# Buffers at multiples of 512 bytes and a reordered lead-in, in a fused retention and feed-forward kernel

## The chip, the cores and the metric

The kernel runs on one core of one Trainium2 chip. The metric is device time in microseconds (us) of one execution. Every time below comes with its number of runs. Every ratio is of executions in the fast state alone, against the kernel before, run on the same chip in the same rounds. Stages and waits are read from one profiled execution of each kernel.

## The reference, cut to what matters

Eight batches of eight heads, 576 positions of 64 elements, are put through retention: scores are `q·k`, scaled by 1/8, multiplied by a decay gamma^(i-j) where i is at or after j, and multiplied with v. The result is laid out as 4608 rows of 512 and goes through `gelu(x @ w_in) @ w_out` with 2048 inner columns, where gelu is `h * sigmoid(1.702 h)`. Inputs and output are float32.

```python
scores = scale * np.matmul(q, k.transpose(0, 1, 3, 2))
ret = scores * Dmat[None, :, :, :]          # Dmat: gamma ** (i - j), 0 above the diagonal
x = np.matmul(ret, v)                       # ... transposed to (4608, 512)
h = x @ w_in
out = (h * (1.0 / (1.0 + np.exp(-1.702 * h)))) @ w_out
```

## The kernel before

The 4608 rows are 36 units of 128 rows, and four units are a chunk. Each unit has its k, q, v loaded (k and q cast to bf16 on the way), k and q transposed, scores, masked scores (`pm`), the retention state (`kv`), and x. Each chunk has `up` (w_in, 16 groups of four matmuls, gelu on ScalarE) and `down` (w_out, four output tiles of 16 matmuls). From chunk 1 on, the attention of the next units is threaded between the matmuls of the present chunk. The part before chunk 1 is the lead-in.

First, the buffers. They are allocated in the order of these lines, and small tables come first, so in the compiled program every large buffer starts 160 bytes past a multiple of 512.

```python
dmat = sb("dmat", [P, P], FP32)
ident = sb("ident", [P, P], BF16)
# ... 13 more small or middling tables ...
kqn = [sb(f"kqn{i}", [P, 2, H, DH], BF16) for i in range(NLD)]   # NLD = 12 slots
vn = [sb(f"vn{i}", [P, H, DH], FP32) for i in range(NLD)]
# ... vp, kqT, pm, kv, xT ...
w_in_sb = sb("w_in_sb", [P, 4, FF], BF16)
w_out_sb = sb("w_out_sb", [P, NF, DM], BF16)
```

Second, the lead-in, in program order (each engine takes its own instructions from it in this order):

```python
def lead_in():
    load_kq(0, 0); load_kq(0, 1); load_v(0, eng="sp")
    # ... iotas ...
    load(1); load_win(0); load(2); load(3)
    for i in range(1, 4): load_win(i)
    for i in range(4): load_wout(i)
    for u in range(4, NPE + 2): load(u)      # units 4 to 9
    warm(8)                                   # eight 512-column matmuls on zeros
    # ... tables ...
    transposes(0, "E", "B")                   # k into PSUM bank E, q into bank B
    # ... scores and block of units 0 and 1 ...
    up(0, 0, 0, 2)                            # first gelu: 256 columns, bank A
    transposes(2, "E", "B")
    up(0, 1, 0, 2)                            # bank B
    # ...
```

Third, units 8 and up are transposed by DMA instead of TensorE, and their loads are held back by that:

```python
for c in range(1, NCH):
    if c == 1:
        for u in range(10, 14):
            load(u, after=["T1_0"])           # until the DMA transpose of unit 9 has landed
    for u in range(4 * c + 6, min(4 * c + 10, NU)):
        dma_transpose(u)                      # SP queue
    for u in range(4 * c + 10, 4 * c + 14):
        load(u, after=[f"T{(4 * c + 9) % NQT}_0"])
```

The `work` table says after which quarter of which output tile of chunk 0 the attention of units 4 to 7 comes.

## Time and profile before

The median of three runs was 310.06 us (310.0 to 310.06).

| | before |
|---|---|
| TensorE (PE) busy | 296.5 us of 308.0, 96% |
| clock records (they begin at 5.0 us) | half speed from 8.4 to 28.9 us (20.48 us) |
| first `down` of chunk 0, first `up` of chunk 1 (start records) | 40.10 us, 61.99 us |
| last w_out landed | 39.05 us |
| DMA transpose of unit 13 landed; PE began the pair of units that reads it | 86.66 us; 86.8 us |

From the page of the kernel before, first the span and two rows of the 40 slices (busy tenths of PE, granted clock in tenths), then two rows of the DMA issues (times issued, KB each, median us from issue to landing):

```profile
span 308.0 us, 6292 instructions
...
PE   6779999899999999999999999999999999999996
...
PEclk9556999999999999999999999999999999999999
...
w_out_sb<-in_moe_w_out_dram POOLq DMA_DIRECT2D x4, 512.0 KB, 17.7
...
vn<-in_v_dram POOLq DMA_DIRECT2D x7, 256.0 KB, 21.4
```

Only the first four slices (31 us) are poor, in busy share and in clock. After that PE is full. The next view is of PE's waits in the first 66 us (who waited for whom: us in total, times, longest):

```profile
PE psB L572 <- ACT kqT L402: 2.2, 2, 1.5
PE psB L392 <- DMA kqn<-in_q_dram: 2.0, 2, 1.3
...
PE psC L484 <- ACT kqT L402: 1.0, 2, 0.7
PE psX L468 <- DVE kv L442: 0.7, 1, 0.7
```

The largest is an `up` (L572) that waits for copies of transposes. The timeline shows why (start, duration, engine, line, operation, and in brackets the idle time before it):

```profile
15.39 1.28 ACT L577 ACT_TABLE_LOAD   x1
...
16.68 0.38 ACT L577 ACTIVATE gT<-psA 128x256 bf16<-128x256 f32 x1
16.96 0.59 ACT L402 ACTIVATE kqT<-psE 128x512 bf16<-128x512 bf16 x1
17.27 0.69 DVE L384 TENSOR_TENSOR vp<-vn,vfac 128x512 bf16<-128x512 f32 x1 [2.77 <-DMA vn<-in_v_dram]
17.44 0.60 ACT L402 ACTIVATE kqT<-psB 128x512 bf16<-128x512 bf16 x1
...
18.10 1.03 PE L572 MATMUL psB<-xT,w_in_sb 128*128 128x256 bf16 x4 [1.50 <-ACT kqT L402]
```

The first gelu needs another activation table, the copies of unit 2 queue behind it, and bank B is not free for the second `up` until the second copy is done. Two other things matter in this stretch: v of unit 2 has just landed, and PE runs at half speed.

The loads of units 10 to 13 start when the transpose of unit 9 has landed (59.53 us), take GpSimd 5.4 us of issuing per unit, and end in the transpose of unit 13 at 86.66 us.

### The profile page before, as it was taken

To read this page: it belongs to the slowest core of one execution; us is meant where nothing else is said; L and a number is where in the kernel's file an instruction comes from. 1 tells how busy PE (TensorE), PEld (TensorE's weight loads), DVE (VectorE), ACT (ScalarE), POOL (GpSimd) and SP (SyncE) were. 2 spreads that over 40 slices of the span, in tenths; PEclk is the share of its full clock that TensorE was granted. 3 is DMA by queue.
4 is the path that set the end of the run, shared out by engine and by line. 5 is a ranking of instruction groups with operands and counts; after the bars stand their busy time and mean duration, and the time that the engine had idled before them with its cause. 6 is when DMAs were issued, how large, how long until landed. Compare 5 with 4: busy or idle time off the path is not lost.

```text
span 308.0 us, 6292 instructions
## 1 busy us (share of the span) xinstructions
PE 296.5 (96%) x2664; PEld 142.1 (46%) x2664; DVE 118.0 (38%) x246; ACT 126.2 (41%) x238; POOL 187.3 (61%) x276
## 2 busy tenths in 40 slices
PE   6779999899999999999999999999999999999996
PEld 2446545444544445445444444454445444443344
DVE  3738307845441444134424442344244424410000
ACT  5555734266115611561166116611661166116611
POOL 8999470299669949973994699489909600000000
PEclk9556999999999999999999999999999999999999
DMA  9999999899999969996999699979999760010022
GB/s 101 173 193 205 205 179 204 148 149 146 116 152 179 166 107 144 186 130 116 141 149 172 99 137 178 174 91 169 176 121 113 126 106 0 36 70 34 0 57 81
DMA packets 120396, 40.27 MB, mean 131 GB/s; under 512 B 109296, under 2 KB 113648, under 8 KB 120368
## 3 DMA queue, kind: packets, MB, share of 16 engines
q0 software_dynamic: 84368, 22.82, 71.6%
q1 hardware_dynamic: 36000, 17.05, 26.4%
q8 instruction: 21, 0.34, 0.5%
q14 instruction: 7, 0.06, 0.1%
HBM read 36.70 MB, written 9.44 MB: 150 GB/s over the span
## 4 chain that ended last, share of the span: by engine, by line
PE 92%; DVE 2%; ACT 2%; DMA 2%; POOL 1%; issue 0%; POOLq 0%
PE psA L583 21%; PE psB L572 20%; PE psA L572 20%; PE psB L583 19%; PE psK L430 3%; PE psX L468 2%; DMA kqn<-in_q_dram 2%; ACT kqT L402 1%; POOL kqn L241 1%; PE psY L536 1%; PE psC L484 1%; DVE pm L503 1%; PE psX L536 1%; PE psX L523 1%; PE psE L392 1%; PE psD L495 1%
## 5 line engine op out<-in xcount | busy, mean ns | idle before, releaser
L241 POOL DMA_DIRECT2D kqn<-in_k_dram x94 | 68.3, 807 | 52.5 <-DMA kqT<-kqn 49.5
L572 PE MATMUL psB<-xT,w_in_sb 128*128 128x512 bf16 (+1 forms) x296 | 74.8, 376 | 2.2 <-ACT kqT L402 2.2
L572 PE MATMUL psA<-xT,w_in_sb 128*128 128x512 bf16 (+1 forms) x296 | 74.9, 377 | 0.1
L259 POOL DMA_DIRECT2D vn<-in_v_dram x93 | 68.9, 854 | 3.2 <-issue 3.2
L583 PE MATMUL psA<-w_out_sb,gT 128*128 128x512 bf16 (+1 forms) x304 | 69.9, 374 | 0.0
L583 PE MATMUL psB<-w_out_sb,gT 128*128 128x512 bf16 (+1 forms) x288 | 64.2, 373 | 0.0
L241 POOL DMA_DIRECT2D kqn<-in_q_dram x70 | 57.0, 892 | 0.0
L577 ACT ACTIVATE gT<-psB 128x512 bf16<-128x512 f32 (+1 forms) x74 | 42.9, 580 | 26.9 <-PE psB L572 26.7
L442 DVE CAST kv<-psK 64x256 bf16<-64x256 f32 x56 | 23.6, 422 | 74.9 <-PE psK L430 74.3
L577 ACT ACTIVATE gT<-psA 128x512 bf16<-128x512 f32 (+1 forms) x74 | 42.9, 580 | 20.8 <-PE psA L572 20.6
L572 PEld LDWEIGHTS psA<-xT,w_in_sb 128*128 128x128 bf16 x296 | 26.0, 99 | 36.8 <-ACT gT L577 12.7
L583 PEld LDWEIGHTS psA<-w_out_sb,gT 128*128 128x128 bf16 x304 | 28.2, 98 | 31.1 <-ACT gT L577 1.0
L583 PEld LDWEIGHTS psB<-w_out_sb,gT 128*128 128x128 bf16 x288 | 27.9, 98 | 31.5
L572 PEld LDWEIGHTS psB<-xT,w_in_sb 128*128 128x128 bf16 x296 | 24.7, 99 | 32.7 <-ACT gT L577 10.5
L593 ACT ACTIVATE osb<-psA 128x512 f32<-128x512 f32 x18 | 10.7, 597 | 66.2 <-PE psA L583 66.2
L593 ACT ACTIVATE osb<-psB 128x512 f32<-128x512 f32 (+1 forms) x18 | 10.5, 586 | 48.7 <-PE psB L583 48.7
L511 DVE TENSOR_TENSOR pm<-psB,maskp 128x384 bf16<-128x384 f32 x12 | 6.7, 558 | 38.3 <-PE psB L495 38.3
L384 DVE TENSOR_TENSOR vp<-vn,vfac_s 128x512 bf16<-128x512 f32 x27 | 18.5, 689 | 1.1 <-DMA vn<-in_v_dram 0.6
L430 PE MATMUL psK<-vp,kqn 128*128 128x128 bf16 x128 | 13.3, 230 | 0.0
L430 PEld LDWEIGHTS psK<-vp,kqn 128*128 128x128 bf16 x128 | 9.7, 102 | 6.9 <-issue 0.7
L595 DVE COPY osb<-psA 128x256 f32<-128x256 f32 x1 | 0.4, 425 | 32.5 <-PE psA L583 32.5
L560 DVE TENSOR_TENSOR xT<-psX,gq 128x512 bf16<-128x512 f32 x13 | 8.9, 682 | 5.2 <-PE psX L536 5.2
(89 smaller groups left out, 230.6 us busy)
## 6 DMA issues: line engine op xcount, KB each, us to landing
out_dram<-osb SPq DMA_DIRECT2D x31, 256.0 KB, 2.7
vn<-in_v_dram POOLq DMA_DIRECT2D x60, 64.0 KB, 3.4
vn<-in_v_dram POOLq DMA_DIRECT2D x26, 128.0 KB, 3.9
kqn<-in_q_dram POOLq DMA_DIRECT2D x50, 64.0 KB, 4.2
w_in_sb<-in_moe_w_in_dram POOLq DMA_DIRECT2D x8, 256.0 KB, 9.4
w_out_sb<-in_moe_w_out_dram POOLq DMA_DIRECT2D x4, 512.0 KB, 17.7
kqn<-in_k_dram POOLq DMA_DIRECT2D x60, 32.0 KB, 3.0
vn<-in_v_dram POOLq DMA_DIRECT2D x7, 256.0 KB, 21.4
```

What stands on the lines that cost most here:

```text
L241: e.dma_start(kqn[sl][p0 : p0 + n, which, ds, :], src[b, ss, s0 : s0 + n, :].rearrange("h p d -> p h d"),)
L259: e.dma_start(vn[sl][p0 : p0 + n, ss, :], v[b, ss, s0 : s0 + n, :].rearrange("h p d -> p h d"),)
L384: op(eng, lambda e: e.tensor_tensor(vp[u % NVP].ap(), vn[sl].ap(), (vfac if u < NSW else vfac_s)[:, ty, :, None].to_broadcast([P, H, DH]), ...
L430: op("pe", lambda e, hp=hp: e.matmul(bank["K"][:, P * hp : P * hp + P], kq_pair(u, 0, hp), v_pair(u, hp), start=(c == 0 and hp == 0), stop ...
L442: op("dve", lambda e, dst=dst, src=src: e.tensor_copy(dst, src), reads=["K"], writes=[f"kv{u % NKV}_{hh}"])
L468: op("pe", lambda e, g=g, pb=pb, hh=hh, hp=hp, s=s, uv=uv, t0=t0, n=n: e.matmul(xbank(hh, slot)[64 * pb : 64 * pb + 64, g, t0 : t0 + n], k ...
L511: op("dve", lambda e: e.tensor_tensor(pm[u % 4][hh][:, 0:384].rearrange("p (a i) -> p a i", i=192), ps32(banks[hh])[:, 0:384].rearrange("p ...
L560: op("dve", lambda e: e.tensor_tensor(xT[ch % 2][:, x_tiles(u0, hh), P * jj : P * jj + 2 * P].rearrange("p g (u t) -> p u g t", u=2), ps32 ...
L572: op("pe", lambda e, a=a: e.matmul(bank[b][:, n0:n1], w_in_sb[:, a, P * f : P * f + P], xT[c % 2][:, a, n0:n1], start=(a == 0), stop=(a == ...
L577: op("act", lambda e: e.activation(gT[c % 2][:, f, n0:n1], bank[b][:, n0:n1], AF.Gelu_apprx_sigmoid), reads=[b], writes=[f"g{c % 2}_{f}_{j ...
L583: op("pe", lambda e, f=f: e.matmul(bank[b][:, 0 : n1 - n0], gT[c % 2][:, f, P * r : P * r + P], w_out_sb[:, f, n0:n1], start=(f == 0), sto ...
L593: op("act", lambda e: e.activation(dst, src, AF.Copy), reads=[b], writes=[f"osb{i}_{n0}"])
```

## The change

Its intent: start every DMA target at a multiple of 512 bytes; keep PE's clock up with filler matmuls; take the gelu table load out of the way; and thread the attention of the first eight units better. The diff, cut to its core:

```diff
+        mask, gpow, iota_k           # 384 bytes, rounded up, ahead of ...
+        kqn, vn, w_in_sb, w_out_sb, osb, kqT, vp, pm, kv, xT, gT   # ... all of these, at multiples of 512
+        gq, dmat, iota_c, ident, ... # the tables that no DMA writes
@@ lead_in
+        def gelu_table():
+            op("act", lambda e: e.activation(gT[1][:, 1, 0:4], gT[1][:, 0, 0:4], AF.Gelu_apprx_sigmoid), ...)
-            g_powers()
-            transposes(0, "E", "B")
-            scale_v(0)
             for a in range(4):
                 gq_first(a)
+            g_powers()
+            transpose_pe(0, 0, "E")
+            transpose_copy(0, 0, "E", "act")
+            warm(1)
+            transpose_pe(0, 1, "B")
+            transpose_copy(0, 1, "B", "act")
+            scale_v(0)
+            gq_next(1)
+            warm(1)
             score1(0)
-            transposes(1, "E", "B")
+            ... transposes(1), with warm(2) between k and q ...
+            block1(0)
+            state(0, "act")
             setup_iota_s()
             setup_vfac_s()
-            block1(0)
-            state(0, "act")
+            gelu_table()
             scale_v(1)
-            gq_next(1)
             score1(1)
+            warm(2)
             block1(1)
+            transposes(2, "E", "E")
             state(1, "act")
             up(0, 0, 0, 2)
-            transposes(2, "E", "B")
             up(0, 1, 0, 2)
             ...
+            transposes(3, "E", "E")
             ...
+            up(0, 5, 0, 2)               # ahead of block1(3)
@@ work: scores and blocks of units 4 to 7 one step later each (but for the block of unit 4), the last one at (3, 3)
@@ steady, chunk 1
-                    up(c, f)
+                    if c == 1 and f < 3:
+                        up(c, f, 0, 3)
+                        if f == 2:
+                            for ff in range(3):
+                                up(c, ff, 3, 4, "CDE"[ff])
+                    else:
+                        up(c, f)
```

More of the change, by code (lines that the diff above doesn't have):

```diff
@@ L182, in sb @@
             return es.enter_context(nc.sbuf_tensor(name, shape, dtype))
+        mask = sb("mask", [P, P], BF16)
+        gpow = sb("gpow", [P, 5, 4], FP32)
+        iota_k = sb("iota_k", [P, 5], FP32)
+        kqn = [sb(f"kqn{i}", [P, 2, H, DH], BF16) for i in range(NLD)]
+        vn = [sb(f"vn{i}", [P, H, DH], FP32) for i in range(NLD)]
+        w_in_sb = sb("w_in_sb", [P, 4, FF], BF16)
+        w_out_sb = sb("w_out_sb", [P, NF, DM], BF16)
+        osb = [sb(f"osb{i}", [P, DM], FP32) for i in range(4)]
+        kqT = [sb(f"kqT{i}", [P, 2 * HP, P], BF16) for i in range(NQT)]
+        vp = [sb(f"vp{i}", [P, H, DH], BF16) for i in range(NVP)]
+        pm = [[sb(f"pm{i}_{hh}", [P, HP * P], BF16) for hh in range(2)] for i in range(4)]
+        kv = [sb(f"kv{i}", [P, HP, DH], BF16) for i in range(NKV)]
+        xT = [sb(f"xT{i}", [P, 4, 512], BF16) for i in range(2)]
+        gT = [sb(f"gT{i}", [P, NF, 512], BF16) for i in range(2)]
+        gq = sb("gq", [P, 6, 4, P], FP32)
         dmat = sb("dmat", [P, P], FP32)
+        iota_c = sb("iota_c", [P, P], FP32)
         ident = sb("ident", [P, P], BF16)
-        mask = sb("mask", [P, P], BF16)
         maskc = sb("maskc", [P, P], BF16)
@@ L189, in bass_retnet_parallel__then__act_gelu_quick_kernel @@
         maskpc = sb("maskpc", [P, 192], BF16)
-        iota_c = sb("iota_c", [P, P], FP32)
-        gpow = sb("gpow", [P, 5, 4], FP32)
-        iota_k = sb("iota_k", [P, 5], FP32)
+        vfac = sb("vfac", [P, 5, H], FP32)
+        vfac_s = sb("vfac_s", [P, 5, H], FP32)
+        iota_s = sb("iota_s", [P, 5], FP32)
         lng = sb("lng", [P, 4], FP32)
         lnsc = sb("lnsc", [P, 1], FP32)
-        iota_s = sb("iota_s", [P, 5], FP32)
-        vfac = sb("vfac", [P, 5, H], FP32)
-        vfac_s = sb("vfac_s", [P, 5, H], FP32)
-        gq = sb("gq", [P, 6, 4, P], FP32)
-        kqn = [sb(f"kqn{i}", [P, 2, H, DH], BF16) for i in range(NLD)]
-        vn = [sb(f"vn{i}", [P, H, DH], FP32) for i in range(NLD)]
-        vp = [sb(f"vp{i}", [P, H, DH], BF16) for i in range(NVP)]
-        kqT = [sb(f"kqT{i}", [P, 2 * HP, P], BF16) for i in range(NQT)]
-        pm = [[sb(f"pm{i}_{hh}", [P, HP * P], BF16) for hh in range(2)] for i in range(4)]
-        kv = [sb(f"kv{i}", [P, HP, DH], BF16) for i in range(NKV)]
-        xT = [sb(f"xT{i}", [P, 4, 512], BF16) for i in range(2)]
-        w_in_sb = sb("w_in_sb", [P, 4, FF], BF16)
-        w_out_sb = sb("w_out_sb", [P, NF, DM], BF16)
-        gT = [sb(f"gT{i}", [P, NF, 512], BF16) for i in range(2)]
-        osb = [sb(f"osb{i}", [P, DM], FP32) for i in range(4)]
         bank = {n: es.enter_context(nc.psum_tensor(f"ps{n}", [P, 512], FP32)) for n in "ABCDEXYK"}
@@ L662, in warm @@
         def warm(n):
-            op("dve", lambda e: e.memset(gT[0][:, 0, :], 0.0), writes=["warm"])
             for i in range(n):
                 op("pe", lambda e: e.matmul(
-                    bank["A"].ap(), gT[0][:, 0, 0:P], gT[0][:, 0, :], skip_group_check=True),
+                    bank["A"].ap(), gT[1][:, 0, 0:P], gT[1][:, 0, :], skip_group_check=True),
                    reads=["warm"], writes=["A"])
+        def gelu_table():
+            op("act", lambda e: e.activation(gT[1][:, 1, 0:4], gT[1][:, 0, 0:4], AF.Gelu_apprx_sigmoid),
+               reads=["warm"], writes=["gelu_table"])
         def lead_in():
@@ L684, in lead_in @@
                 load(u)
+            op("dve", lambda e: e.memset(gT[1][:, 0, :], 0.0), writes=["warm"])
             warm(8)
@@ L688, in lead_in @@
             setup_vfac()
-            g_powers()
-            transposes(0, "E", "B")
-            scale_v(0)
             for a in range(4):
                 gq_first(a)
-            score1(0)
-            transposes(1, "E", "B")
+            g_powers()
[7 more added lines that the diff above has]
+            warm(1)
+            score1(0)
+            transpose_pe(1, 0, "E")
+            transpose_copy(1, 0, "E", "act")
+            warm(2)
+            transpose_pe(1, 1, "B")
+            transpose_copy(1, 1, "B", "act")
+            block1(0)
+            state(0, "act")
             setup_iota_s()
             setup_vfac_s()
-            block1(0)
-            state(0, "act")
+            gelu_table()
             scale_v(1)
-            gq_next(1)
             score1(1)
+            warm(2)
             block1(1)
+            transposes(2, "E", "E")
             state(1, "act")
             up(0, 0, 0, 2)
-            transposes(2, "E", "B")
             up(0, 1, 0, 2)
@@ L709, in lead_in @@
             score1(2)
+            transposes(3, "E", "E")
             gq_next(2)
             up(0, 2, 0, 2)
-            transposes(3, "E", "B")
             up(0, 3, 0, 2)
@@ L719, in lead_in @@
             up(0, 4, 0, 2)
+            up(0, 5, 0, 2)
             block1(3)
             state(3, "act")
-            for f in range(5, 8):
+            for f in range(6, 8):
                 up(0, f, 0, 2)
@@ L734, in lead_in @@
                 (1, 1): lambda: (scale_v(4), transposes(4, "E", "E")),
-                (1, 2): lambda: score1(4),
-                (1, 3): lambda: (scale_v(5), transposes(5, "E", "E")),
-                (2, 0): lambda: (block1(4), score1(5), state(4)),
-                (2, 1): lambda: (scale_v(6), transposes(6, "E", "E")),
-                (2, 2): lambda: (block1(5), score1(6), state(5)),
-                (3, 0): lambda: (scale_v(7), transposes(7, "E", "E")),
-                (3, 1): lambda: (block1(6), score1(7), state(6)),
-                (3, 2): lambda: block1(7),
+                (1, 3): lambda: (score1(4), scale_v(5), transposes(5, "E", "E")),
+                (2, 0): lambda: (block1(4), state(4)),
+                (2, 1): lambda: (score1(5), scale_v(6), transposes(6, "E", "E")),
+                (2, 3): lambda: (block1(5), state(5), score1(6)),
+                (3, 0): lambda: (scale_v(7), transposes(7, "E", "E"), state(6)),
+                (3, 2): lambda: (block1(6), score1(7)),
+                (3, 3): lambda: block1(7),
             }
```

## The prediction

> **What bounds the kernel now.** From 62 us on it is TensorE and nothing else: the chain of waits runs through PE alone, the waits view shows none of PE after 63 us, and a 128x512 matmul comes every 0.216 us. The change leaves that part alone; only the time before chunk 1 (its first `up` stands at 62.15 us on the chain) can shrink.
>
> Chunk 0's feed-forward needs 128 matmuls of 512 columns (27.6 us) and eight units' attention about 7 to 9. The rest of the 62 us is:
> - Clock. The records show full speed from 5.0 to 8.4 us, half from 8.4 to 28.9, then full. The half-speed stretch is six times the full one of 3.41 us, in keeping with the window of about 3.4 us of the Trainium skill ("TensorE: Matmul & The Clock Gate", What's actually happening). From 10 to 25 us PE is 70 to 85% busy (windows).
> - One stall (timeline): gelu table load (1.28 us at 15.4), two transpose copies behind it, bank B held by them; the second `up` waits 1.50 us.
> - Loads. DVE waits for v of unit 2 until 17.27; k, q, v of unit 3 land at 18.2, 19.1, 20.8, the second quarter of w_in at 23.0, the last of w_out at 39.05 (needed near 42.9).
> - At 59 to 62 us PE waits about 1.4 us for DVE.
>
> **What the change does, costed.**
> 1. Fillers (6 matmuls, 0.22 or 0.43 us each) and denser order. Activity before 8.4 us hardly rises: the gq activations (1.64 us) now precede the first transpose copies, so unit 0's scores start near 8.2 us instead of 7.4. I expect half speed until 12 or 19 us, not 29.
> 2. The table load moves to about 12.6 us, beside waiting; transposes of units 2 and 3 leave bank B. PE's waits of 1.5 and 0.75 us go.
> 3. Units 4 to 7 are spread, and the first three `up` of chunk 1 do three quarters first: 1.4 us of waits goes, 0.3 us of small matmuls comes.
> 4. Alignment. k and q packets (128 B) take 32 ns, v's of 4096 B often 313 but sometimes 165; weights read near 414 GB/s and can't gain. The skill's "DMA: Bandwidth & Descriptors" (Specifications) says writes under 512 B cost a read-modify-write; nothing in this trace shows an effect of alignment. I give 60% to a gain of 10 to 40% on k, q and v.
>
> **Sum (estimates from those durations).** Without any DMA gain I place chunk 0's full-width `up` at about 29 us (33.2 now), w_out's last landing then costs 0.7 us, and chunk 1 starts 5 us earlier: 305. With faster loads, units 2 and 3 land 1.5 to 3 us sooner, w_out 2 us: 302.5. Slow clock until 29 us: 307.
>
> Prediction 303.8 us, 8 in 10 between 301 and 307.5. Faster by over 2%: 0.5; within 2%: 0.49; slower: 0.01.
>
> **What would show it.** Clock records: full speed from 19 us or earlier. Waits: no `up` waits for transpose copies; table load before the first `up`. Timeline: full-width `up` at 26 to 29 us, first `down` at 33 to 36. DMA: k/q packets under 32 ns, v3 landing before 19 us. After 62 us: 0.216 us per matmul as now; PE's waits near 60 us gone.
>
> **What would make it wrong.** The clock at half through 29 us; alignment worth more or nothing; a new wait for w_out or units 4 to 7, whose loads had only 4 us of slack.

## The result, and the profile after

The changed kernel took 305.04 us (median of 4 runs, 304.5 to 305.65), the kernel before 310.03 us (4 runs, 309.72 to 310.06). The ratio is 0.9842 (95% interval 0.9822 to 0.9862). A ratio here is the mean time of one kernel's fast runs over that of the other's of the same rounds, so not quite the ratio of the medians. That is 1.6% faster, inside the predicted range and in the class "within 2%".

The same rows of the page after:

```profile
span 302.7 us, 6295 instructions
...
PE   6599999999999999999999999999999999999996
...
PEclk9979999999999999999999999999999999999999
...
w_out_sb<-in_moe_w_out_dram POOLq DMA_DIRECT2D x4, 512.0 KB, 15.5
...
vn<-in_v_dram POOLq DMA_DIRECT2D x7, 256.0 KB, 17.6
```

The clock is at half speed for one window only (15.4 to 18.8 us, 3.41 us by the records). w_out lands 2.2 us sooner after its issue, v 3.8 us. PE's waits in the first 66 us:

```profile
PE psE L392 <- DMA kqn<-in_k_dram: 1.7, 2, 1.2
PE psX L523 <- DVE pm L503: 1.4, 1, 1.4
...
PE psC L484 <- ACT kqT L402: 0.8, 1, 0.8
PE psB L392 <- DMA kqn<-in_q_dram: 0.6, 1, 0.6
```

No `up` waits for transpose copies any more; instead PE waits for k of unit 2 and for masked scores of units 1 and 3. The timeline of the same work as above:

```profile
12.42 1.28 ACT L669 ACT_TABLE_LOAD   x1
...
15.82 0.61 PE L392 MATMUL psE<-ident,kqn 128*128 128x128 bf16 x4 [0.44 <-DMA kqn<-in_q_dram]
...
16.47 1.08 ACT L402 ACTIVATE kqT<-psE 128x512 bf16<-128x512 bf16 x2 [2.55 <-PE psE L392]
...
17.51 1.06 PE L572 MATMUL psB<-xT,w_in_sb 128*128 128x256 bf16 x4
18.22 0.38 ACT L577 ACTIVATE gT<-psA 128x256 bf16<-128x256 f32 x1
```

The table load fills time in which ScalarE waited anyway, the copies come before the first gelu, and the second `up` follows the first without a wait.

The start records give where the 5.3 us of the profiled span (308.0 to 302.7) came from. Half speed is the time at half clock before the last matmul.

| us from the span's start | before | after | earlier by |
|---|---|---|---|
| first `down`, chunk 0 | 40.10 | 35.76 | 4.34 |
| first `up`, chunk 1 | 61.99 | 56.53 | 5.46 |
| first `down`, chunk 1 | 77.21 | 71.90 | 5.31 |
| first `up`, chunk 2 | 93.52 | 88.21 | 5.31 |
| end | 307.99 | 302.67 | 5.32 |
| half speed | 20.48 | 3.41 | |

So 4.3 us come before the first `down`, 1.1 us between it and chunk 1, and nothing after. The windows view tells what the 4.3 us are made of. It counts busy time in a stretch; the first row of each kernel is the time up to its first `down`, the second its half-speed stretch. After the length of the stretch comes PE's busy time, with the number of its instructions; PEclk is the mean granted clock.

```profile
core 0: us, PE busy (x) PEld busy (x) DVE busy (x) ACT busy (x) POOL busy (x), PEclk, DMA share, GB/s
0.00:40.10 40.10, 32.67 (x240) 18.01 (x241) 20.45 (x55) 23.70 (x65) 33.93 (x49) 0.74 1.38 176
8.39:28.87 20.48, 16.36 (x143) 9.99 (x144) 12.72 (x29) 10.78 (x31) 20.48 (x27) 0.50 1.37 185
```

```profile
0.00:35.76 35.76, 28.29 (x244) 15.96 (x247) 20.30 (x55) 23.68 (x66) 33.24 (x48) 0.95 1.31 177
15.43:18.84 3.41, 3.02 (x24) 2.24 (x24) 0.69 (x1) 2.34 (x6) 3.41 (x6) 0.50 1.70 226
```

PE idled as long after as before (35.76 less 28.29 is 7.5 us, 40.10 less 32.67 is 7.4). The new order moved its waits and did not shorten their sum. What fell is PE's busy time, by 4.4 us although six filler matmuls came in, and of that time the part at half clock fell from 16.36 to 3.02 us. In this account the lead-in's gain is faster matmuls.

On its face this says: lead-in, done. The experiments show that it is not the whole of it.

### The profile page after: what moved, and what is told of

Read it like the earlier page. It is cut to its first block, busy times and chain, and to the rows that moved or that the text cites. A ratio compares the mean times of both kernels' runs of the same rounds, so it can differ in the third digit from the quotient of the medians.

```text
span 302.7 us, 6295 instructions
## 1 busy us (share of the span) xinstructions
PE 288.9 (95%) x2646; PEld 140.6 (46%) x2682; DVE 117.9 (39%) x246; ACT 126.4 (42%) x242; POOL 187.6 (62%) x276
## 4 chain that ended last, share of the span: by engine, by line
PE 91%; DMA 2%; POOL 2%; DVE 2%; issue 2%; POOLq 0%
PE psA L583 21%; PE psB L572 20%; PE psA L572 20%; PE psB L583 20%; DMA kqn<-in_q_dram 2%; PE psK L430 2%; PE psX L468 2%; POOL kqn L241 1%; PE psE L392 1%; PE psY L536 1%; DVE pm L503 1%; PE psX L536 1%; PE psD L495 1%; PE psB L495 1%; PE psC L484 1%
## 5 line engine op out<-in xcount | busy, mean ns | idle before, releaser
L572 PE MATMUL psA<-xT,w_in_sb 128*128 128x512 bf16 (+2 forms) x287 | 72.7, 371 | 0.9 <-ACT gT L577 0.3
L572 PE MATMUL psB<-xT,w_in_sb 128*128 128x512 bf16 (+2 forms) x289 | 72.3, 372 | 0.4
L583 PE MATMUL psA<-w_out_sb,gT 128*128 128x512 bf16 (+1 forms) x288 | 66.3, 373 | 2.3 <-issue 2.2
L577 ACT ACTIVATE gT<-psB 128x512 bf16<-128x512 f32 (+2 forms) x74 | 42.8, 579 | 24.8 <-PE psB L572 24.6
L577 ACT ACTIVATE gT<-psA 128x512 bf16<-128x512 f32 (+2 forms) x74 | 42.7, 577 | 19.8 <-PE psA L572 19.7
L402 ACT ACTIVATE kqT<-psE 128x512 bf16<-128x512 bf16 x14 | 7.7, 593 | 10.9 <-PE psE L392 10.9
```

The lines of the kernel that those rows point to most:

```text
L402: op("act", lambda e: e.activation(dst, src, AF.Copy), reads=[b], writes=[f"T{u % NQT}_{which}"])
L572: op("pe", lambda e, a=a: e.matmul(bank[b][:, n0:n1], w_in_sb[:, a, P * f : P * f + P], xT[c % 2][:, a, n0:n1], start=(a == 0), stop=(a == ...
L577: op("act", lambda e: e.activation(gT[c % 2][:, f, n0:n1], bank[b][:, n0:n1], AF.Gelu_apprx_sigmoid), reads=[b], writes=[f"g{c % 2}_{f}_{j ...
L583: op("pe", lambda e, f=f: e.matmul(bank[b][:, 0 : n1 - n0], gT[c % 2][:, f, P * r : P * r + P], w_out_sb[:, f, n0:n1], start=(f == 0), sto ...
```

## The experiments

Theory A: PE's lead-in (order, and perhaps clock) is what was lost, and the layout adds little. Rival B: the layout earns most. Rival C: the clock earns most. Twelve kernels ran, all correct. Their times and ratios:

| run | median us (runs) | kernel before, same rounds | ratio |
|---|---|---|---|
| align_only | 309.04 (6) | 309.66 | 0.9976 |
| reorder_only | 309.06 (6) | 309.66 | 0.9970 |
| fillers_only | 309.65 (6) | 309.66 | 0.9999 |
| no_fillers | 305.17 (5) | 309.66 | 0.9856 |
| old_unpaced | 315.62 (6, two slow) | 309.98 | 1.0156 |
| v_aligned | 306.74 (4) | 309.98 | 0.9886 |
| sp_v | 304.45 (4) | 309.98 | 0.9828 |
| sp_v_unpaced | 306.01 (6, one slow) | 309.98 | 0.9856 |
| old_leadin | 308.12 (6) | 309.73 | 0.9944 |
| old_downs | 305.97 (4) | 309.73 | 0.9874 |
| stall_back | 305.39 (4) | 309.73 | 0.9855 |
| by_need | 309.17 (6) | 309.73 | 0.9984 |

And the start records of their profiled runs, with before and after for comparison:

| | first `down`, chunk 0 | first `up`, chunk 1 | first `down`, chunk 1 | first `up`, chunk 2 | end | half speed |
|---|---|---|---|---|---|---|
| before | 40.10 | 61.99 | 77.21 | 93.52 | 307.99 | 20.48 |
| align_only | 39.58 | 61.46 | 76.68 | 93.00 | 307.45 | 17.07 |
| reorder_only | 35.91 | 56.67 | 72.04 | 93.27 | 307.73 | 10.24 |
| fillers_only | 40.28 | 62.16 | 77.38 | 94.28 | 308.82 | 17.07 |
| no_fillers | 35.96 | 56.73 | 72.09 | 88.41 | 302.90 | 10.24 |
| v_aligned | 36.53 | 57.30 | 72.67 | 90.60 | 305.06 | 3.41 |
| sp_v | 35.61 | 56.38 | 71.74 | 88.06 | 302.55 | 3.41 |
| old_leadin | 39.38 | 60.15 | 75.51 | 91.83 | 306.27 | 17.07 |
| old_downs | 35.67 | 57.56 | 72.78 | 89.09 | 303.55 | 6.83 |
| stall_back | 36.67 | 57.44 | 72.81 | 89.12 | 303.58 | 6.83 |
| by_need | 38.33 | 59.10 | 74.47 | 90.79 | 305.28 | 3.41 |
| after | 35.76 | 56.53 | 71.90 | 88.21 | 302.67 | 3.41 |

### align_only: the layout alone

```diff
 kernel before
-        the old order of the buffers
+        the new order of the buffers
```

> The kernel before with nothing but the new order of the buffers. Theory A (the gain is TensorE's lead-in: clock and order; loads only bind a little): v packets of 4096 B fall from 313 to about 165 ns, the last w_out lands near 37 us instead of 39.05, but PE's chain is held elsewhere, so the time falls by 0 to 0.7 us (309.3 to 310.0). Rival B (the layout earns most of the 5 us): the time falls by 2.5 us or more.

Ratio 0.9976, about 0.7 us, with an interval that just touches 1 (0.9951 to 1.0002). Theory A's mechanism and size hold here: v's packets fell to 168 ns (median), the last w_out landed at 37.26 us, and the first `down` moved by 0.5 us only. Taken alone, the layout looks like nearly nothing.

### reorder_only: everything but the layout

```diff
 changed kernel
-        the new order of the buffers
+        the old order of the buffers
```

> The changed kernel with the old order of the buffers. Theory A: v packets at 313 ns again, units 4 to 7 land 2 to 4 us later, w_out last near 39 us; PE comes to the last quarter of the first output tile at about 38.5 us and waits about 0.5 us, unit 2 and 3 come 0.2 to 1.2 us later: the time is 0.5 to 2 us above the changed kernel, 305.5 to 307. Rival B: 307.5 or more.

This is the miss that changed the theory. The ratio is 0.9970 (0.9936 to 1.0004): without the layout the reorder earns 0.9 us, not 4. So "layout alone" and "reorder alone" are worth 0.7 and 0.9 us, neither told from nothing, and both together 4.9 us (0.0158 of 310 us). By its number (307.5 or more) the run falls to rival B. Yet B is not right either: align_only did not earn most, and the lead-in of this run is as early as that of the changed kernel: the second table has its first `down` at 35.91 us and chunk 1 at 56.67 us, 5.3 us earlier than before. The gain was there and was given back inside chunk 1, between 72.04 and 93.27 us: 21.2 us where every other kernel of this set but those with late transposes has 16.3. PE's waits over that run name it:

```profile
PE psD L495 <- DMA kqT<-kqn: 2.8, 2, 1.8
```

And the timeline and the chain that ended last, at those two places:

```profile
74.56 0.24 PE L495 MATMUL psD<-kqT 64*64 64x128 bf16 x1 [0.98 <-DMA kqT<-kqn]
...
85.05 0.24 PE L495 MATMUL psD<-kqT 64*64 64x128 bf16 x1 [1.85 <-DMA kqT<-kqn]
```

```profile
75.30 2.48 POOL kqn L241 x4
77.78 4.11 DMA kqn<-in_q_dram
...
81.95 3.05 DMA kqT<-kqn
...
85.05 0.22 PE psD L495
```

PE waits for the DMA transposes of units 11 and 13. In the kernel before, unit 13's landed at 86.66 us and PE came at 86.8; here it landed at 85.00 us and PE would have come at about 83. The chain is one of loads: units up to 9 land, unit 9 is transposed, GpSimd issues units 10 to 13 at 5.4 us each, unit 13 is transposed. With PE's waits the clock also fell to half once more, from 85.99 to 89.40 us by the records; PE was busy all through this window of 3.41 us, so it lost 1.7 us there, and 2.8 and 1.7 are most of the 4.9 us (an estimate worked out from these records).

Where does the layout come in? It shortens exactly this chain, in the part up to unit 9. Loads and transposes landed as follows:

| landed, us | before | reorder_only | align_only | after |
|---|---|---|---|---|
| last w_out | 39.05 | 37.77 | 37.26 | 36.99 |
| last part of q of unit 9 | 56.31 | 55.32 | 51.65 | 52.08 |
| transpose of unit 9 | 59.53 | 58.50 | 56.47 | 55.06 |
| transpose of unit 13 | 86.66 | 85.00 | 82.61 | 81.60 |
| PE began the scores of units 12 and 13 | 86.8 | 82.9 | 86.3 | 81.5 |

The layout alone brings the transpose of unit 13 4 us forward, for a PE that comes only 0.5 us sooner. The reorder alone brings PE 4 us forward, for a transpose that comes only 1.7 us sooner. Both together meet again, with no slack to speak of. This is theory D of the later runs: two chains of nearly equal length, of which either alone can't be shortened to effect.

### fillers_only and no_fillers: the clock

```diff
 fillers_only: kernel before (no_fillers: the same four lines taken out of the changed kernel)
+            warm(1)   # between the k and the q transposes of unit 0
+            warm(1)   # before the scores of unit 0
+            warm(2)   # between the k and the q transposes of unit 1
+            warm(2)   # after the scores of unit 1
```

> The kernel before with only the six filler matmuls, at the same places in the order. Theory C (the clock is what was lost): full speed from 5 us on or at most one half-speed window, and 2 to 4 us less. Theory A' (order and clock each need the other: at full speed PE only waits longer for the table load and for bank B, since transposes and activations stand in its way until 22 us): half speed much shorter in the records, but only 0.5 to 2 us less.

> The changed kernel without its six filler matmuls. Theory C: the clock record shows half speed from 8.4 us to beyond 20 us and the time rises by 2 us or more. Theory A': the clock drops at 8.4 us, is at half for 7 to 14 us, but until 16 us PE waits for loads anyway, so the time rises by 0.5 to 1.5 us.

Fillers alone: 0.9999 (0.9979 to 1.0019). Both theories for this run missed, A' (0.5 to 2 us less) and C (2 to 4 us less). But in the old order the fillers did not keep the clock up: the records of the profiled run show half speed for 17.07 us, until 27.8 us. So the run shows that the fillers earn nothing there. It does not show what a fast clock would earn.

Fillers taken away from the changed kernel: 0.9856 against 0.9842, some 0.4 us with overlapping intervals (0.9834 to 0.9878 and 0.9822 to 0.9862). The profiled run without them had three half-speed windows (9.2 to 19.5 us) instead of one, and its first `down` was 0.2 us later. The expectation for no_fillers (0.5 to 1.5 us) was a little high. A likely reason is that up to 16 us PE waits for loads and for VectorE anyway (the last such wait of that stretch ended at 15.90 us). Rival C falls as far as the fillers go, and no further.

The rest of the clock is not settled. In the kernel before the clock stayed at half until 28.9 us, in no_fillers until 19.5 us, in reorder_only until 17.7 us. So the early rise goes with the new order, without the fillers and without the layout too; that the order's density brings it is argued, not shown. It is also most of the gain that the traces show: up to the first `down` PE was busy for 32.67 us in the kernel before and for 29.08 us in no_fillers (16.36 and 7.77 us of it at half clock), and idle for 7.43 and 6.88 us. So 3.6 of these 4.1 us are busy time and 0.6 us are waits. This is an account and no test: I have no run with the new order and a slow clock from 19 to 29 us, nor one with the old order and a fast clock. The record holds a warning, too. Of the 33 executions of the kernel before beside these runs, 12 are listed with a mean clock of 0.999 or 1.000, and they took 309.71 to 310.92 us, no less than the other 21 (0.966 to 0.989; 308.72 to 311.47 us). Either their clock records are incomplete, as those of one execution of sp_v_unpaced were (last section), or PE waited longer at full clock. Their traces were not kept.

### old_leadin, old_downs, stall_back: which part of the order

```diff
 old_leadin: changed kernel
-        the lead-in from setup_vfac to the first up of columns 256 to 511
+        the same stretch of the kernel before (old order, no fillers, no gelu_table, banks E and B)
 old_downs: changed kernel
-        the new work table, the split products of chunk 1
+        the old work table, up(c, f) throughout
 stall_back: changed kernel
-            gelu_table()
-            transposes(2, "E", "E"), transposes(3, "E", "E")
+            transposes(2, "E", "B"), transposes(3, "E", "B")
```

> The changed kernel (new buffers, new work table, split first products of chunk 1) with the lead-in of before up to the first `up` of columns 256 to 511: old order, no fillers, table load at the first gelu, transposes of units 2 and 3 in banks E and B. Theory: the first output product starts at 39.6 us as in the layout-alone kernel, 3.8 later than in the changed one; the rest of the change saves about 1.1 us after it; so 307.5 to 308.5. Rival (the downstream part earns most): 306 or less.

> The changed kernel with the old work table between the output products of chunk 0 and without the split of chunk 1's first products. Theory: lead-in as in the changed kernel (first output product at 35.8 us), then 21.9 us instead of 20.8 to chunk 1's first product, the waits of about 1.4 us for DVE near 55 us are back: 305.6 to 306.5. Rival: no difference, 305.

> The changed kernel with the table load back at the first gelu and the transposes of units 2 and 3 back in banks E and B, but the new order kept. Theory G (the stall was the order: in the new order the copies go before the gelu, so the table load hits nothing): first output product 0.2 to 1 us later, time 0.2 to 1 us up. Theory H (table load and bank cost 2 us or more by themselves): first output product at 38 us or later, 307 or more.

All three came out within what was expected. With the layout in place, undoing the lead-in costs 0.0102 of the time (0.9944 against 0.9842), 3.2 us; undoing the work table and the split costs 0.0032, 1.0 us; and the layout itself is the first 0.7 us. Those three add up to the whole 4.9 us, but only with the layout put in first: taken out last, out of the whole, the layout costs 4.0 us (0.9970 against 0.9842). In the traces, old_leadin has its first `down` at 39.38 us and old_downs takes 21.89 us from there to chunk 1 instead of 20.77.

stall_back decides for theory G against H: the table load and bank B, put back into the new order, cost 0.9 us at the first `down` and 0.4 us of the time (0.9855, 0.9839 to 0.9872, against 0.9842, so not clear of noise). The stall of the kernel before needed the old order. In the new order the copies of unit 2 stand ahead of the first gelu, so a late table load delays little. The 0.9 us are not a wait: PE idled 6.28 us up to the first `down` of stall_back and 7.47 us in the changed kernel, but was busy at half clock for 5.47 against 3.02 us. Which step of the new order earns most was not separated.

What changed before chunk 1 is seen in the chain that ended last, of before and then of after, at unit 7 (start, us, what):

```profile
57.75 0.76 DVE xT L550 x2
58.50 1.19 DVE pm L503 x2
59.70 0.33 DVE kv L442
60.05 0.44 DVE kv L442
```

```profile
54.29 0.76 DVE xT L550 x2
55.05 1.21 DVE pm L503 x2
...
56.30 0.30 PE psY L523 x4
56.60 0.76 PE psA L572 x4
```

The copies of the state (kv) are gone from it; x and the masked scores (pm) are still on it. PE's own waits there fell from 0.96 us (0.74 and 0.22, for kv) to 0.17 us (for pm).

### v_aligned: which buffers feel the alignment

```diff
 changed kernel
+        pad0 = sb("pad0", [P, 80], BF16)      # 160 bytes
         kqn = [...]
+        pad1 = sb("pad1", [P, 176], BF16)     # 352 bytes: vn and all after it back at a multiple of 512
         vn = [...]
```

> The changed kernel with only the k and q buffers moved to 160 bytes past a multiple of 512; v, weights and outputs stay at multiples. Theory F (only the 4096 B packets of v feel the alignment): v packets about 165 ns, k and q packets 32 ns, time as the changed kernel, 304.5 to 306. Rival (k and q matter too): 307 or more, loads of unit 9 land after 53 us.

The packets behaved as theory F says. From the packet records, before 60 us:

| median ns of a packet | before | reorder_only | v_aligned | align_only | after |
|---|---|---|---|---|---|
| k, q: 128 B | 32 | 32 | 32 | 32 | 32 |
| weights: 1024 B | 98 | 98 | 98 | 98 | 98 |
| v: 4096 B (16 pieces of 256 B) | 283 | 266.5 | 173 | 168 | 168 |

In the two kernels of the old layout v's packets fall into two groups, near 161 and near 313 ns; in the new one the second is gone (2% of them at 280 ns or more, before 52%). But the time did not follow: 0.9886 (0.9858 to 0.9914), 306.74 us, 1.4 us above the changed kernel by the ratios and between what I expected of F (up to 306) and of its rival (307 or more). The profiled run lost it in the same place as reorder_only, a wait of 1.4 us for the transpose of unit 13, which landed at 84.03 us. So k and q may matter too, but by which way is not shown. The loads were already up to 1.2 us later in this run by unit 7 (v of unit 7 at 48.65 us, in the changed kernel 47.48), and the last part of q of unit 9 was 2.2 us later (54.30 and 52.08). The transposes do not settle it. The 256 B packets of those of units 8 and 9 took 43.5 ns on average, in the changed kernel 27.4. But in reorder_only, with k and q at the same offset, they took 27.0, in no_fillers, with k and q aligned, 31.7, and the median is 18 ns in all four.

### old_unpaced, sp_v, sp_v_unpaced, by_need: loosening the loads another way

These four test theory D by relieving the load chain without the layout, and look for a faster kernel.

```diff
 old_unpaced: reorder_only            (sp_v_unpaced: the same in sp_v)
-            load(u, after=["T1_0"])   # units 10 to 13
+            load(u)
 sp_v: changed kernel
+            v of units 1 to 3 from the SP queue, right after that of unit 0; k and q as before
 by_need: changed kernel
+            v of units 1, 2, 3 from the SP queue, after q of units 0, 1, 2 has landed
+            k and q of unit 2 ahead of the first quarter of w_in
```

> The changed kernel with the old order of the buffers (309.06 us as reorder_only), and the loads of units 10 to 13 no longer held back until the transposes of unit 9. Theory D (two chains of equal length: the reorder shortens PE's, but loads of units 10 to 13, held until unit 9 is in, were just in time before and now are 3.5 us late, whatever the alignment): with the loads let go earlier PE's two waits of 2.8 us for transposes near 75 and 85 us vanish and the time is 304.5 to 306, with no alignment at all. Rival E (alignment itself makes reads and writes cheaper for PE or the DMA in the whole run): it stays at 308 to 309.

> The changed kernel with v of units 1 to 3 issued at the start from the SP queue, beside that of unit 0. Theory D: GpSimd's issues come 2.7 us earlier, unit 2 and 3 and w_out land 1 to 2.5 us earlier and the first output product starts near 33 us, but loads of units 10 to 13 have no slack in the changed kernel (the last transposes land at 81.6 us, scores follow at 81.5), and they come earlier by about as much as the lead-in's loads do: 303 to 304.5. Rival: nothing changes, 305.

> The same with the loads of units 10 to 13 let go at once. Theory D: neither chain holds the other, 302 to 303.5, faster than both kernels. If loads are not what binds the lead-in: 304.5 to 305.

> The changed kernel with k and q of unit 2 loaded before the first quarter of w_in, and v of units 1 to 3 from the SP queue, each let go when q of the unit before has landed. Theory (loads bind the lead-in, and the last transposes for chunk 1 are just in time): q of unit 2 lands near 13 us instead of 15.8, first output product at 33 to 35 us, the transposes of unit 13 land near 80 us; 303 to 304.3, faster than the changed kernel, part of the lead-in's gain lost again to that wait. Rival: 305, no gain.

old_unpaced missed by 10 us, in the wrong direction: 1.0156. The hold on units 10 to 13 is not idle. Without it their loads are in flight during the transposes of units 8 and 9: unit 8's was issued at 54.2 us and landed at 66.1 us (in reorder_only 52.4 and 57.1), and k and q packets, 32 ns on average in reorder_only, took 48 ns from 57 to 90 us. PE waited 6.0 us in all for transposes. So it confirms that late transposes stop PE there, but as a test of D it failed, since it lengthened the chain that it was meant to shorten. Part of its loss is also in the lead-in, which the edit doesn't touch (first `down` at 38.76 us, after a wait of 2.4 us for w_in; reorder_only waited 1.5 us there). I put that down to a spread in the loads from run to run; it was not tested.

sp_v lands within the time that was expected (303 to 304.5 us), but cannot be told from the changed kernel: 0.9828 (0.9795 to 0.9860) against 0.9842. Loads came earlier (last w_out 35.34 us, transpose of unit 13 at 79.74 us), but the first `down` did not (35.61 us, expected near 33), so that step of the expectation failed. The three extra loads of v ran beside k and q of units 0 and 1, and q of unit 1 landed at 11.82 us instead of 8.40; k of unit 2, which PE waits for next, was not earlier.

sp_v_unpaced is a miss as well: theory D expected 302 to 303.5 us, and the fast runs took 304.63 to 306.31 us (0.9856). Its profiled execution was slow (see the last section) and is not used. So both forecasts that theory D made by letting the loads go failed. What stands for the two chains are PE's waits for the transpose of unit 13 in reorder_only and v_aligned.

by_need missed: 0.9984, nearly all of the gain lost (307.08 to 310.58 us over its executions; the profiled one was the fastest of them). q of unit 2 did land early, at 12.34 us, but everything behind it came later: q of unit 3 at 20.64 us (18.26 in the changed kernel), the last w_out at 39.18 (36.99). From the SP queue v moves in 1024 packets of 256 B, and between 12 and 22 us these took 30.8 ns each; spread over 16 engines that is 2.0 us for one v. From GpSimd's queue v moves in 64 packets of 4096 B, 176 ns each in the same stretch, which is 0.7 us (estimates worked out from the packet records). Two v in that stretch and one before it, at 22.8 ns a packet, make some 3 us of DMA time more, and the loads behind them lost 2.2 to 2.4 us. That this is the cause is argued from these numbers; no run separated it.

No version clearly beat the changed kernel.

## Why the prediction was right, point by point

The number was right: 305.04 us measured, 303.8 predicted, range 301 to 307.5, and it fell into "within 2%", to which the prediction gave 0.49. Several of its steps were not right, and that the number held is in part luck: the reorder was put at 5 us by itself and gave 0.9, the layout at 2.5 us on top of it and gave 4.0, and the two errors partly cancelled.

1. **"From 62 us on it is TensorE and nothing else ... only the time before chunk 1 can shrink".** This is the step that failed. It is true that PE waited for nobody there before the change. But absence of a wait was read as slack. The transpose of unit 13 was in at 86.66 us for a PE that came at 86.8. reorder_only shows what follows: chunk 1 begins 5.3 us earlier and 4.9 us of it are lost to that chain.
2. **"Without any DMA gain ... chunk 1 starts 5 us earlier: 305".** The first half held: 5.3 us without the layout. The second did not: 309.06 us. The lead-in and the end of the kernel are not joined by PE alone.
3. **"With faster loads, units 2 and 3 land 1.5 to 3 us sooner, w_out 2 us: 302.5".** w_out did (2.06 us, of which 1.28 came in reorder_only already, without the layout). Units 2 and 3 did not: q of unit 2 by 0.17 us, v of unit 3 by 1.16 us (20.83 to 19.67). The expected gain of 10 to 40% on k, q and v came for v alone (a median packet 283 to 168 ns), while k and q stayed at 32 ns. In PE's lead-in the layout was worth 0.15 us on top of the reorder (35.91 to 35.76), not 2.5 us. Its 4.0 us came behind the lead-in, by the chain of point 1.
4. **Clock.** "Half speed until 12 or 19 us, not 29" was right: one window, over at 18.8 us. Of the two causes that it gave, fillers and a denser order, the fillers are not needed (no_fillers: full clock from 19.5 us) and are worth some 0.4 us, not clear of noise. The weight of the clock was right: in the traces the lead-in's gain is PE's busy time and not its waits. Steps of 3.41 us run through all records (3.41, 6.83, 10.24, 17.07 and 20.48 us are 1, 2, 3, 5 and 6 of them), as the Trainium skill's page "TensorE: Matmul & The Clock Gate" (What's actually happening) leads one to expect.
5. **The table load and bank B.** Right as far as the waits go: the load moved to 12.4 us, PE's waits for copies at the first `up` went. But as many waits came elsewhere (7.4 us of idle time before, 7.5 after), and stall_back adds that the table load and the bank alone are worth little. The 1.28 us of one load agrees with "ScalarE: Activation LUTs" (What ACT_TABLE_LOAD costs), which has 1283 ns for the load alone.
6. **Units 4 to 7 and the split.** Right: 1.4 less 0.3 us expected, 1.1 us measured in the traces, 1.0 us by old_downs.
7. **The marks.** First `down` at 33 to 36 us: 35.76. Full-width `up` (512 columns) at 26 to 29 us: 29.07, at the edge. k and q packets under 32 ns: missed, 32. PE's waits near 60 us gone: 0.17 of 0.96 us left. v of unit 3 before 19 us: missed, 19.67. Later chunks run as before: from the first `up` of chunk 2 to that of chunk 3 is 30.72 us in both kernels (93.52 to 124.24 and 88.21 to 118.93).
8. **What would make it wrong.** I named new waits for w_out or for units 4 to 7. A new wait for loads did lie in ambush, but for the second round of them.

## What to carry to other kernels

An engine that never waits has not thereby a supplier with slack: before shortening the engine's own chain, compare when each input landed with when it was first read, and do it for stages far behind the edit. Where two chains are equal, each part of a change measured alone looks worthless and the two together are worth their full sum, so test the parts by taking them out of the whole as well as by adding them to the old kernel. A hold on a load can be there to protect another transfer; see what shares the DMA engines before letting it go. And add up an engine's idle time before crediting a new order with fewer waits: here the sum stayed and the busy time fell.

## What the Trainium skill lacked or had wrong

- "DMA: Bandwidth & Descriptors" has no account of what the start of an SBUF target does to write speed. Here 4096 B packets of v, written as 256 B pieces to buffers at 160 bytes past a multiple of 512, often took 313 ns, and at multiples of 512 mostly 168 ns. Its section "How a descriptor splits into AXI transactions" describes a cost of starts off 256 B, for reads; were it the same for writes, a 256 B piece that straddles such a boundary would need two transactions, which would fit a factor of 1.9. The runs did not test that reason, and the start alone does not decide: v of units 1, 4 and 8 took about 170 ns in the kernel before too, and v of unit 7 took 314 ns there but 173 in reorder_only, at the same start.
- The same page (Specifications) says that writes under 512 B cost a read-modify-write. The 128 B packets of k and q took 32 ns at either layout, so alignment neither removed nor added anything to see; the runs can't confirm or deny the reason.
- The same page (Issuing engine by pattern) calls the SP and ScalarE queues generally faster. In packet time, loads of v were costlier that way: 1024 packets of 256 B at 30.8 ns against 64 of 4096 B at 176 ns (12 to 22 us of by_need and of the changed kernel).
- No page tells how much other loads stretch a DMA transpose: unit 8's took 4.6 us from issue to landing in reorder_only and 12 us in old_unpaced, with loads beside it.
- "TensorE: Matmul & The Clock Gate" (Seeing it yourself) says that clock records can't always be trusted; it does not tell of an execution that has none. One execution of sp_v_unpaced took 774.16 us. Its trace holds no clock record at all (the profile then prints a clock of 1.000), yet its matmuls of 512 columns came every 0.62 us instead of every 0.22 us, and chunk 1 took 83.5 us (113.02 to 196.54 us) instead of 31.7. The other executions of that kernel took 304.63 to 306.31 us. The cause stays open.
